# Computing each distance once in the position-bias stage of an attention and cos-gated FFN kernel

## The chip, the core and the metric

One core of a Trainium2 chip runs the whole program. The metric is the device time of one execution in microseconds (us); the kernel before has a median of 800.36 us over three runs (799.08 to 800.66).

The engines have short names in the profile: PE is TensorE's matmul, PEld its weight load, DVE is VectorE, ACT is ScalarE, POOL is GpSimd, SP is SyncE, which here only issues DMAs.

## What is computed

Attention with a learned bias that depends on the distance of two positions, then a feed-forward layer. S is 576, there are 8 heads and a batch of 4; all data are float32.

```
rel = pos[:, None] - pos[None, :]
psi_rel = log1p(abs(rel));  psi_i = log1p(max(pos[:, None], 1))
x = (psi_rel / psi_i)[..., None]
bias = max(x @ w1 + b1, 0) @ w2                  # 32 hidden values, 8 heads
scores = 0.125 * q @ k.T + bias
attn = softmax(scores);  y = attn @ v
h = y @ w_in;  out = (h * cos(h)) @ w_out
```

For a row i the bias depends on abs(i - j) alone, and on i by the factor 1 / psi_i.

## The kernel before

The program has three stages one after another: the bias stage, attention over 16 units (head pair and batch), and the feed-forward layer. The change touches the first alone.

**The bias stage** makes, for each row i and head, one line that holds the negative bias for every distance, and writes it to a scratch tensor `sc` in DRAM; attention reads it back (`load_bias`) at an offset that depends on the row. Rows go in 36 groups of 16. In the order of work groups 0 to 7 are rows 0 to 127 (t = 0), 8 to 15 the next 128 (t = 1), 16 to 19 the last 64 rows (t = 4), 20 to 27 and 28 to 35 the two tiles between (t = 2, 3); `qi` names a group by its rows, `k` (or `n` in the loop) by its place in this order. For group `qi` the distances forward reach `nf = 576 - 16 qi`, those backward `nr = 16 qi + 15`; together they are 591 columns, and the larger of the two, `n`, runs from 304 to 576.

A group has four subgroups `s` of four rows. Partitions hold 4 rows by 32 hidden values. For each `s`:

- one instruction makes the hidden values `ht` from the table `lt` of log1p(distance): on DVE (line 301, a multiply by the row's column `sl` of `st_` and a max against `nb1`), on POOL for `s == 2` of groups 8, 12, ... 32 (also line 301), or on ACT for `s == 3` of three groups in four (line 303, a Relu with a scale column and a bias column);
- TensorE multiplies by `nbd` (line 306). Its 32 output columns make it a matmul on one quarter of the array, `tile_position=(0, 32 * s)`, and its output goes to partitions 32 s to 32 s + 31 of the PSUM tile `pa`. The line is made in two or three pieces (`cuts`): the backward distances with a reversed operand, the forward ones as they are, and a further cut where a PSUM bank ends at 512 columns. Each float32 matmul runs as two passes, which the trace records as two matmuls with two weight loads.

When the four are done ACT adds a constant and writes the 591 columns from PSUM to `rt` (`bias_store`, line 318), and SP issues the DMA to `sc` (line 319).

Each engine runs its own instructions in the order in which the loop at line 328 writes them: group n's `ht` and matmuls, then the store of group n - 1, then, for n = 11 to 15, `turn`: transposes of the first unit's k and q on TensorE with copies out of PSUM on ACT (`kN`, `qT`, lines 195 to 212). POOL's queue also holds the splits of q and k (lines 172 and 176) at n = 1 and n = 16. Buffers tie the engines together: 2 PSUM tiles `pa` (each of two banks), 9 buffers for `ht`, 5 for `rt`.

Of the kernel before, what the change touches and what calls it, by code (L numbers as in the profile page):

```python
# [28 lines left out]
def kernel(  # L29
# [80 lines left out]
    with tc.manual_schedule():  # L110
# [152 lines left out]
        ha = opened(stage, "ha", 9, "left")  # L263
# [6 lines left out]
        st_ = ca.tile([128, S // 4], F32, name="st_")  # L270
        nb1 = ca.tile([128, 1], F32, name="nb1")
# [8 lines left out]
        nc.vector.tensor_scalar(st_, mi, w1c, None, ALU.mult)  # L280
        nc.vector.tensor_scalar(nb1, b1c, -1.0, None, ALU.mult)
# [6 lines left out]

        def bias_rows(k, t, gi):
# [4 lines left out]
            base = 512 - nr if max(nf, nr) <= 512 else 0  # L294
            cuts = sorted({0, nr, nr + nf} | ({512 - base} if base + nr + nf > 512 else set()))
            for s in range(4):
                ht = ha.tile([128, S], F32, tag="h", name="ht")
# [513 lines left out]
```

## Time and profile before

| what | value |
|---|---|
| median of three runs | 800.36 us |
| the profiled execution, its own time | 803.56 us |
| its span, first to last instruction | 801.7 us |
| granted TensorE clock over the span | 0.995 |
| PE, DVE, ACT, POOL busy | 764.9, 598.4, 459.1, 415.4 us |
| bias stage: first `ht`, last store starts | 4.80 and 79.54 us |
| attention, then feed-forward | to about 395, then to 801.7 us |

Busy times are those of the whole span. TensorE is busy for 95% of it, but its matmuls overlap, so the share doesn't tell how fast a stage goes; for the bias stage the distance between two stores `rt` is the better clock. The timeline merges instructions of the same line and tiles that follow each other closely into one row with a count. "idle before" names what the engine waited for.

### The profile page before, as it was taken

To read this page: it belongs to the slowest core of one execution; us is meant where nothing else is said; L and a number is where in the kernel's file an instruction comes from. 1 tells how busy PE (TensorE), PEld (TensorE's weight loads), DVE (VectorE), ACT (ScalarE), POOL (GpSimd) and SP (SyncE) were. 2 spreads that over 40 slices of the span, in tenths; PEclk is the share of its full clock that TensorE was granted. 3 is DMA by queue.
4 is the path that set the end of the run, shared out by engine and by line. 5 is a ranking of instruction groups with operands and counts; after the bars stand their busy time and mean duration, and the time that the engine had idled before them with its cause. 6 is when DMAs were issued, how large, how long until landed. Compare 5 with 4: busy or idle time off the path is not lost.

```text
span 801.7 us, 14168 instructions
## 1 busy us (share of the span) xinstructions
PE 764.9 (95%) x4882; PEld 619.2 (77%) x4882; DVE 598.4 (75%) x1300; ACT 459.1 (57%) x964; POOL 415.4 (52%) x493
## 2 busy tenths in 40 slices
PE   7899899989999999899999999999999999999997
PEld 4335677767777777677889998898888888889996
DVE  8558576757676767677577978889899898986655
ACT  5548677767777766676656555554544445443332
POOL 3324466656575657576753744637355373644400
PEclk9999999999999999999999999999999999999999
DMA  4647734673466346632001010111101011001112
GB/s 153 194 148 249 181 77 107 164 145 76 120 173 133 94 123 160 135 81 58 19 26 52 28 53 27 52 41 39 53 26 54 27 53 36 18 14 53 45 48 79
DMA packets 70599, 68.50 MB, mean 85 GB/s; under 512 B 30080, under 2 KB 54784, under 8 KB 70528
## 3 DMA queue, kind: packets, MB, share of 16 engines
q1 hardware_dynamic: 70528, 67.60, 31.1%
q8 instruction: 39, 0.64, 0.3%
q14 instruction: 32, 0.26, 0.1%
HBM read 42.00 MB, written 15.61 MB: 72 GB/s over the span
## 4 chain that ended last, share of the span: by engine, by line
PE 81%; ACT 7%; DMA 4%; DVE 4%; issue 3%; POOL 2%; SPq 0%; POOLq 0%; DVEq 0%; ACTq 0%
PE ph L613 24%; PE po L668 23%; PE pv L494 10%; PE s L378 8%; PE pa L306 7%; PE pt L437 4%; PE pt L195 3%; ACT P L408 3%; DMA bt<-sc 3%; POOL ht L301 1%; ACT kN L202 1%; PE pt L442 1%; ACT wb L91 1%; ACT PT L450 1%; DMA kS<-kN 1%
## 5 line engine op out<-in xcount | busy, mean ns | idle before, releaser
L430 POOL TENSOR_SCALAR P<-P,rc 128x576 f32<-128x576 f32 x144 | 111.1, 783 | 86.8 <-ACT PT L450 23.6
L389 DVE CUSTOM_DVE_ANT_0 neg<-s,bt 128x576 f32<-128x576 f32 x144 | 103.8, 753 | 37.4 <-PE s L378 33.3
L617 ACT ACTIVATE a<-ph,quarter 128x384 int32<-128x384 f32 x96 | 55.8, 581 | 106.6 <-PE ph L613 105.5
L408 ACT ACTIVATE P<-neg,m 128x576 f32<-128x576 f32 x144 | 110.6, 775 | 9.8 <-DVE dn L420 5.7
L480 POOL TENSOR_TENSOR xs<-xT,xs 128x384 fp32r<-128x384 f32 x96 | 107.7, 1122 | 8.0
L613 PE MATMUL ph<-xs,wpre 128*128 128x384 f32 x576 | 109.4, 338 | 0.8 <-DVE a L632 0.8
L613 PE MATMUL ph<-xs,w 128*128 128x384 f32 x576 | 108.3, 337 | 0.5 <-DVE a L632 0.5
L623 DVE SCALAR_TENSOR_TENSOR r<-a,ph 128x384 f32<-128x384 int32 x96 | 52.9, 551 | 73.1 <-ACT a L617 73.0
L613 PEld LDWEIGHTS ph<-xs,wpre 128*128 128x128 f32 x576 | 101.8, 188 | 6.2 <-DVE a L632 2.1
L613 PEld LDWEIGHTS ph<-xs,w 128*128 128x128 f32 x576 | 101.3, 188 | 5.6 <-DVE a L632 1.6
L628 ACT ACTIVATE r<-r,hpi 128x384 f32<-128x384 f32 x96 | 59.4, 619 | 69.4 <-DVE r L624 69.4
L378 PE MATMUL s<-kN,qT 128*128 128x288 f32 x320 | 94.3, 317 | 2.6 <-DVE dn L420 2.2
L378 PE MATMUL s<-kS,qT 128*128 128x288 f32 x320 | 87.1, 295 | 0.0
L437 PE MATMUL pt<-ident,P 128*128 128x128 f32 x576 | 80.7, 279 | 6.5 <-POOL P L430 6.4
L479 POOL TENSOR_SCALAR xs<-xT 128x384 fp32r<-128x384 f32 x96 | 62.0, 646 | 39.7 <-PE ph L613 39.7
L494 PE MATMUL pv<-PT,vN 128*64 128x320 f32 (+1 forms) x512 | 76.0, 419 | 0.0
L668 PE MATMUL po<-w,gh 128*128 128x512 f32 x288 | 75.3, 396 | 0.0
L668 PE MATMUL po<-wpre,gh 128*128 128x512 f32 x288 | 75.2, 396 | 0.0
L642 DVE TENSOR_TENSOR gl<-a,gh 128x384 fp32r<-128x384 f32 x96 | 74.4, 775 | 0.6 <-ACT gh L636 0.6
L306 PE MATMUL pa<-ht,nbd 128*32 128x79 f32 (+43 forms) x640 | 67.9, 419 | 6.1 <-POOL ht L301 3.6
L378 PEld LDWEIGHTS s<-kN,qT 128*128 128x128 f32 x320 | 60.9, 190 | 16.4 <-issue 9.7
L453 DVE COPY PT<-pt 128x512 f32<-128x512 f32 x64 | 43.8, 684 | 39.9 <-PE pt L437 39.8
(82 smaller groups left out, 1385.9 us busy)
## 6 DMA issues: line engine op xcount, KB each, us to landing
sc<-rt SPq DMA_DIRECT2D x36, 295.5 KB
kS<-kN SPq DMA_DIRECT2D x32, 304.0 KB
raw<-in_moe_w_in_dram SPq DMA_DIRECT2D x16, 512.0 KB
raw<-in_moe_w_out_dram SPq DMA_DIRECT2D x16, 512.0 KB
bt<-sc SPq DMA_DIRECT2D x16, 288.0 KB
nk<-in_k_dram SPq DMA_DIRECT2D x32, 128.0 KB
nq<-in_q_dram SPq DMA_DIRECT2D x32, 128.0 KB
vN<-in_v_dram SPq DMA_DIRECT2D x32, 128.0 KB
```

The lines of the kernel that those rows point to most:

```text
L306: nc.tensor.matmul(ps[32 * s : 32 * s + 32, base + a : base + b], nbd, rhs, start=True, stop=True, tile_position=(0, 32 * s),)
L378: nc.tensor.matmul(s[:, hf, 0:HALF], a, kt[u][:, c0 : c0 + HALF], start=(n == 0), stop=(n == 2 * len(stats) - 1),)
L389: nc.vector.tensor_tensor_reduce(neg, s[:, :, 0:HALF], bias[hp, t, h].rearrange("p (a x) -> p a x", a=2), 1.0, 3.0e38, ALU.add, ALU.min, m ...
L408: nc.scalar.activation(out=P[u, j][:, 576 * h : 576 * h + 576], in_=neg.rearrange("p a x -> p (a x)"), func=AF.Exp, bias=m[:, 0:1], scale= ...
L430: nc.gpsimd.tensor_scalar(p, p, r, 1.0, ALU.mult, ALU.mult)
L437: nc.tensor.transpose(ps[:, 128 * c : 128 * c + 128], p[:, o : o + 128], ident)
L479: nc.gpsimd.tensor_scalar(h, src, 1.0, 1.0, ALU.mult, ALU.mult)
L480: nc.gpsimd.tensor_tensor(l, src, f(h), ALU.subtract)
L494: nc.tensor.matmul(ps[64 * h : 64 * h + 64, 0 : WQ[hf]], a, m, start=(c == 0), stop=(c == 4), tile_position=(0, 64 * h), skip_group_check= ...
L613: nc.tensor.matmul(ps, a, x, start=(i == 0), stop=(i == 3 * KD - 1))
L642: nc.vector.tensor_tensor(gl, a, f(G[key][0]), ALU.subtract)
L668: nc.tensor.matmul(O[n][i], a[:, 128 * i : 128 * i + 128], w, start=(i0 == 0 and p == 0), stop=(i0 == GF - 1 and p == 2),)
```

## The change

Since a row's factor 1 / psi_i is positive, it can be taken out of the activation: max(w1 x + b1, 0) becomes the factor times max(w1 lt + b1 psi_i, 0). The change uses this:

- `lt` is multiplied by w1 once. The hidden values need one limit per row, `edge` (or `nedge` on ACT), in place of a factor and a limit: DVE and POOL run a max with one column (line 313), ACT a Relu with a bias column (line 315).
- TensorE computes columns 0 to n - 1 alone, each distance once, in one piece, or two where n is over 512 (line 318).
- `bias_store` runs two activations, forward and reversed, on the same PSUM columns, with the row's factor as the scale column `mrow` and the constant as the bias column (line 334).
- ACT makes `ht` for `s == 3` of every second group instead of three in four; DVE makes the others.
- At the start DVE computes `edge`, `nedge` and `mrow`; `mrow` needs four small matmuls with a selection matrix `pick`.
- `ht` has 8 buffers instead of 9.

```diff
-        ha = opened(stage, "ha", 9, "left")
+        ha = opened(stage, "ha", 8, "left")
...
-        nc.vector.tensor_scalar(st_, mi, w1c, None, ALU.mult)
-        nc.vector.tensor_scalar(nb1, b1c, -1.0, None, ALU.mult)
+        nc.vector.reciprocal(nedge, mi)
+        nc.vector.tensor_scalar(nedge, nedge, b1c, None, ALU.mult)
+        nc.vector.tensor_scalar(edge, nedge, -1.0, None, ALU.mult)
+        nc.vector.tensor_scalar(lt, lt, w1c, None, ALU.mult)
...
+        nc.vector.tensor_copy(
+            pick.rearrange("p (g h) -> p g h", g=4), ident[:, 0:128:32].unsqueeze(2).to_broadcast([128, 4, 8])
+        )
+        pm = bank()
+        for s in range(4):
+            nc.tensor.matmul(
+                pm[32 * s : 32 * s + 32, 0:NQ], pick, mi[:, s : 4 * NQ : 4], start=True, stop=True, tile_position=(0, 32 * s)
+            )
+        nc.vector.tensor_copy(mrow, pm[:, 0:NQ])
...
-                if s < 3 or k % 4 == 2:
+                o = 4 * qi + s
+                if s < 3 or k % 2:
                     eng = nc.gpsimd if s == 2 and k in POOL_H else nc.vector
-                    eng.tensor_scalar(ht[:, 0:n], lt[:, 0:n], sl, nb1, ALU.mult, ALU.max)
+                    eng.tensor_scalar(ht[:, 0:n], lt[:, 0:n], edge[:, o : o + 1], None, ALU.max)
                 else:
-                    nc.scalar.activation(out=ht[:, 0:n], in_=lt[:, 0:n], func=AF.Relu, scale=sl, bias=b1c)
-                for a, b in zip(cuts[:-1], cuts[1:]):
-                    rhs = ht[:, nr - a : nr - b : -1] if b <= nr else ht[:, a - nr : b - nr]
+                    nc.scalar.activation(out=ht[:, 0:n], in_=lt[:, 0:n], func=AF.Relu, bias=nedge[:, o : o + 1])
+                for a in range(0, n, 512):
+                    b = min(a + 512, n)
...
-            nc.scalar.activation(out=rt[:, 0 : RB - 1], in_=ps, func=AF.Identity, bias=cst[:, int(k % 4 == 2) : int(k % 4 == 2) + 1])
+            c = cst[:, k % 2 : k % 2 + 1]
+            for o, i in ((rt[:, nr : nr + nf], ps[:, 0:nf]), (rt[:, 0:nr], ps[:, nr:0:-1])):
+                nc.scalar.activation(out=o, in_=i, func=AF.Identity, scale=mrow[:, qi : qi + 1], bias=c)
```

Three places of the order show what the diff alone doesn't. TensorE's queue at group 16, the first of t = 4, with the transposes of q ahead of it, before:

```order
L195 MATMUL pt_548<-identr_64,sq_211 128x128 x4
L306 MATMUL pa_554<-ht_555,nbd_136 32x512 [waits DVE_49,PE_49,Activation_49]
L306 MATMUL pa_554<-ht_555,nbd_136 32x15
L306 MATMUL pa_554<-ht_555,nbd_136 32x64
L306 MATMUL pa_554<-ht_560,nbd_136 32x512 [waits DVE_49]
L306 MATMUL pa_554<-ht_560,nbd_136 32x15
```

and now:

```order
L195 MATMUL pt_510<-identr_64,sq_215 128x128 x4
L318 MATMUL pa_516<-ht_517,nbd_136 32x512 [waits DVE_49,PE_49,Activation_49]
L318 MATMUL pa_516<-ht_517,nbd_136 32x16
L318 MATMUL pa_516<-ht_521,nbd_136 32x512 [waits DVE_49]
L318 MATMUL pa_516<-ht_521,nbd_136 32x16
L318 MATMUL pa_516<-ht_525,nbd_136 32x512 [waits Pool_49]
```

A subgroup had three pieces here (six passes in the trace) and has two (four passes). In groups 4 to 15 and 20 to 35 it had two and has one.

ACT's queue around the copies of k (n = 11 and 12), before:

```order
L318 ACTIVATE rt_430<-pa_393,cst_137 128x591 [waits DMAHW3_49,PE_49,Activation_49]
L202 ACTIVATE kN_438<-pt_439 128x2x2x128 [waits PE_49]
L303 ACTIVATE ht_458<-lt_132,pk_133,st__134 128x384 [waits DVE_49]
L318 ACTIVATE rt_462<-pa_413,cst_137 128x591 [waits DMAHW4_49,Activation_49]
L202 ACTIVATE kN_438<-pt_465 128x2x2x128 [waits PE_49]
L211 ACTIVATE kN_438<-pt_471 128x128 [waits PE_49]
L212 ACTIVATE kN_438<-pt_471 128x64
L303 ACTIVATE ht_491<-lt_132,pk_133,st__134 128x368 [waits DVE_49]
L318 ACTIVATE rt_495<-pa_445,cst_137 128x591 [waits DMAHW5_49,Activation_49]
```

and now:

```order
L334 ACTIVATE rt_403<-pa_373,cst_137,mrow_154 128x416 [waits DMAHW3_49,PE_49]
L334 ACTIVATE rt_403<-pa_373,cst_137,mrow_154 128x175
L202 ACTIVATE kN_412<-pt_413 128x2x2x128 [waits PE_49]
L315 ACTIVATE ht_429<-lt_132,nedge_135 128x384 [waits Activation_49]
L334 ACTIVATE rt_432<-pa_390,cst_137,mrow_154 128x400 [waits DMAHW4_49]
L334 ACTIVATE rt_432<-pa_390,cst_137,mrow_154 128x191
L202 ACTIVATE kN_412<-pt_436 128x2x2x128 [waits PE_49]
L211 ACTIVATE kN_412<-pt_442 128x128 [waits PE_49]
L212 ACTIVATE kN_412<-pt_442 128x64
L334 ACTIVATE rt_462<-pa_419,cst_137,mrow_154 128x384 [waits DMAHW5_49]
L334 ACTIVATE rt_462<-pa_419,cst_137,mrow_154 128x207
```

Each store is two rows; the `ht` of group 13 (368 columns) is no longer between the copies and the next store, DVE makes it.

DVE's queue from the arrival of `pack` to the second `ht`, before:

```order
L280 TENSOR_SCALAR st__134<-pk_133 128x144 [waits DMAHW0_49]
L281 TENSOR_SCALAR nb1_135<-pk_133 128x1
L282 TENSOR_SCALAR nbd_136<-pk_133 128x32
L285 MEMSET cst_137 128x2
L286 TENSOR_SCALAR cst_137<-pt_157 96x1 [waits DVE_49,PE_49]
L287 TENSOR_SCALAR cst_137<-pt_157 128x1
L301 TENSOR_SCALAR ht_163<-lt_132,st__134,nb1_135 128x576 [waits DMAHW1_49]
L301 TENSOR_SCALAR ht_168<-lt_132,st__134,nb1_135 128x576
```

and now:

```order
L282 RECIPROCAL nedge_135<-pk_133 128x144 [waits DMAHW0_49]
L283 TENSOR_SCALAR nedge_135<-nedge_135,pk_133 128x144 [waits DVE_49]
L284 TENSOR_SCALAR edge_134<-nedge_135 128x144 [waits DVE_49]
L285 TENSOR_SCALAR lt_132<-lt_132,pk_133 128x576 [waits DMAHW1_49]
L286 TENSOR_SCALAR nbd_136<-pk_133 128x32
L289 MEMSET cst_137 128x2
L290 TENSOR_SCALAR cst_137<-pt_161 96x1 [waits DVE_49,PE_49]
L291 TENSOR_SCALAR cst_137<-pt_161 128x1
L293 COPY pick_155<-ident_63 128x32
L301 COPY mrow_154<-pt_167 128x36 [waits PE_49]
L313 TENSOR_SCALAR ht_174<-lt_132,edge_134 128x576
L313 TENSOR_SCALAR ht_178<-lt_132,edge_134 128x576
```

Seven instructions stand between the arrival of `lt` and the first `ht`, one of them behind a wait for TensorE.

## Rows read from the trace of the kernel before

**Rows 1.** Busy time by stretch: PE, PEld, DVE, ACT, POOL (instructions), clock, DMA share, GB/s

```profile
4.80:24.60 19.80, 16.17 (x168) 9.82 (x168) 18.03 (x34) 11.51 (x16) 10.97 (x7) 1.00 0.48 154
24.60:43.35 18.75, 18.05 (x146) 8.41 (x147) 11.15 (x23) 10.84 (x21) 6.22 (x4) 0.91 0.64 212
43.35:56.61 13.26, 13.26 (x98) 4.69 (x100) 5.57 (x11) 5.02 (x8) 2.49 (x3) 1.00 0.28 95
56.61:79.55 22.94, 22.32 (x257) 11.46 (x247) 20.19 (x43) 18.34 (x28) 9.26 (x6) 1.00 0.71 249
```

**Rows 2.** Timeline of ACT, the stores of groups 8, 15 and 19: start, duration

```profile
26.56 0.75 ACT L318 ACTIVATE rt<-pa,cst 128x591 f32<-128x591 f32 x1 [4.30 <-issue]
...
43.35 0.74 ACT L318 ACTIVATE rt<-pa,cst 128x591 f32<-128x591 f32 x1
...
56.61 0.75 ACT L318 ACTIVATE rt<-pa,cst 128x591 f32<-128x591 f32 x1 [2.27 <-issue]
```

**Rows 3.** Timeline of TensorE's weight loads in group 16

```profile
42.88 0.17 PEld L306 LDWEIGHTS pa<-ht,nbd 128*32 128x32 f32 x5 [0.32 <-issue]
43.34 0.11 PEld L306 LDWEIGHTS pa<-ht,nbd 128*32 128x32 f32 x1 [0.29 <-issue]
43.77 0.17 PEld L306 LDWEIGHTS pa<-ht,nbd 128*32 128x32 f32 x5 [0.32 <-issue]
```

**Rows 4.** Timeline of TensorE's matmuls in group 14: start, time to the last one's end

```profile
37.43 1.22 PE L306 MATMUL pa<-ht,nbd 128*32 128x239 f32 x16
```

**Rows 5.** Groups of instructions by shape, 0 to 110 us: busy us, mean ns of one

```profile
L318 ACT ACTIVATE rt<-pa,cst 128x591 f32<-128x591 f32 x36 | 27.0, 751 | 24.2 <-PE pa L306 11.0 <-issue 9.8 <-ACT ht L303 1.8
L408 ACT ACTIVATE P<-neg,m 128x576 f32<-128x576 f32 x14 | 10.8, 772 | 3.5 <-DVE m L389 2.7 <-DVE dn L420 0.8
L303 ACT ACTIVATE ht<-lt,pk,st__134 128x576 f32<-128x576 f32 x2 | 1.7, 862 | 2.7 <-DMA lt<-in_ltab_dram 2.7
L303 ACT ACTIVATE ht<-lt,pk,st__134 128x320 f32<-128x320 f32 x2 | 1.3, 642 | 0.0
L301 DVE TENSOR_SCALAR ht<-lt,st__134,nb 128x576 f32<-128x576 f32 x6 | 3.3, 579 | 1.7 <-DMA lt<-in_ltab_dram 0.9 <-PE pa L306 0.8
L301 DVE TENSOR_SCALAR ht<-lt,st__134,nb 128x304 f32<-128x304 f32 x7 | 2.9, 438 | 4.9 <-PE pa L306 4.9
L306 PE MATMUL pa<-ht,nbd 128*32 128x335 f32 x8 | 1.5, 457 | 0.0
L306 PE MATMUL pa<-ht,nbd 128*32 128x336 f32 x8 | 1.5, 446 | 0.0
```

**Rows 6.** Timeline of ACT, store and hidden values back to back

```profile
15.17 0.75 ACT L318 ACTIVATE rt<-pa,cst 128x591 f32<-128x591 f32 x1
15.82 0.79 ACT L303 ACTIVATE ht<-lt,pk,st__134 128x496 f32<-128x496 f32 x1
```

**Rows 7.** Timeline of ACT, the copies of k in groups 11 and 12

```profile
31.60 0.66 ACT L202 ACTIVATE kN<-pt 128x512 fp32r<-128x512 f32 x1 [1.08 <-PE pt L195]
...
34.56 0.65 ACT L202 ACTIVATE kN<-pt 128x512 fp32r<-128x512 f32 x1 [1.09 <-PE pt L195]
```

**Rows 8.** Timeline of POOL, hidden values of groups 8 and 32, split of k

```profile
18.76 5.81 POOL L301 TENSOR_SCALAR ht<-lt,st__134,nb 128x448 f32<-128x448 f32 x1 [7.18 <-ACT rt L318]
...
42.52 1.89 POOL L176 TENSOR_TENSOR sk<-nk,sk 128x320 fp32r<-128x320 f32 x2
...
71.44 2.45 POOL L301 TENSOR_SCALAR ht<-lt,st__134,nb 128x464 f32<-128x464 f32 x1 [3.60 <-DVE ht L301]
```

**Rows 9.** Timeline of DVE from the arrival of `pack`

```profile
3.06 0.30 DVE L280 TENSOR_SCALAR st__134<-pk 128x144 f32<-128x144 f32 x1 [0.71 <-DMA pk<-in_pack_dram]
...
4.80 18.03 DVE L301 TENSOR_SCALAR ht<-lt,st__134,nb 128x576 f32<-128x576 f32 x34 [0.88 <-DMA lt<-in_ltab_dram]
```

**Rows 10.** DVE's reciprocals in attention: ns min/median/max

```profile
L423 DVE RECIPROCAL rc<-dn x80: 162/166/168, 83.9 to 386.1; 128x2 f32<-128x2 f32 x64, 128x1 f32<-128x1 f32 x16
```

**Rows 11.** Chain that ended last: start, us, what

```profile
87.38 6.89 DMA bt<-sc
```

More of the change, by code (lines that the diff above doesn't have):

```diff
@@ L269 @@
         pk = ca.tile([128, pack.shape[1]], F32, name="pk")
-        st_ = ca.tile([128, S // 4], F32, name="st_")
-        nb1 = ca.tile([128, 1], F32, name="nb1")
+        edge = ca.tile([128, S // 4], F32, name="edge")
+        nedge = ca.tile([128, S // 4], F32, name="nedge")
         nbd = ca.tile([128, 32], F32, name="nbd")
@@ L279 @@
         bd, w2r = pk[:, 146:178], pk[0:C, 178:306]
-        nc.vector.tensor_scalar(st_, mi, w1c, None, ALU.mult)
-        nc.vector.tensor_scalar(nb1, b1c, -1.0, None, ALU.mult)
+        mrow = ca.tile([128, NQ], F32, name="mrow")
+        pick = ca.tile([128, 32], F32, name="pick")
+        nc.vector.reciprocal(nedge, mi)
+        nc.vector.tensor_scalar(nedge, nedge, b1c, None, ALU.mult)
+        nc.vector.tensor_scalar(edge, nedge, -1.0, None, ALU.mult)
+        nc.vector.tensor_scalar(lt, lt, w1c, None, ALU.mult)
         nc.vector.tensor_scalar(nbd, bd, -1.0, None, ALU.mult)
@@ L293, in bias_rows @@
             ps = ps_a.tile([128, 1024], F32, tag="a", name="pa")
-            base = 512 - nr if max(nf, nr) <= 512 else 0
-            cuts = sorted({0, nr, nr + nf} | ({512 - base} if base + nr + nf > 512 else set()))
             for s in range(4):
                 ht = ha.tile([128, S], F32, tag="h", name="ht")
-                sl = st_[:, 4 * qi + s : 4 * qi + s + 1]
-                if s < 3 or k % 4 == 2:
+                o = 4 * qi + s
+                if s < 3 or k % 2:
                     eng = nc.gpsimd if s == 2 and k in POOL_H else nc.vector
-                    eng.tensor_scalar(ht[:, 0:n], lt[:, 0:n], sl, nb1, ALU.mult, ALU.max)
+                    eng.tensor_scalar(ht[:, 0:n], lt[:, 0:n], edge[:, o : o + 1], None, ALU.max)
                 else:
-                    nc.scalar.activation(out=ht[:, 0:n], in_=lt[:, 0:n], func=AF.Relu, scale=sl, bias=b1c)
-                for a, b in zip(cuts[:-1], cuts[1:]):
-                    rhs = ht[:, nr - a : nr - b : -1] if b <= nr else ht[:, a - nr : b - nr]
+                    nc.scalar.activation(out=ht[:, 0:n], in_=lt[:, 0:n], func=AF.Relu, bias=nedge[:, o : o + 1])
+                for a in range(0, n, 512):
+                    b = min(a + 512, n)
                     nc.tensor.matmul(
-                        ps[32 * s : 32 * s + 32, base + a : base + b],
+                        ps[32 * s : 32 * s + 32, a:b],
                         nbd,
-                        rhs,
+                        ht[:, a:b],
                         start=True,
@@ L313, in bias_rows @@
                     )
-            return ps[:, base : base + nr + nf]
+            return ps
         def bias_store(k, t, gi, ps):
+            qi = groups[t][gi]
+            nf, nr = S - 16 * qi, 16 * qi + 15
             rt = ra.tile([128, RB], F32, tag="r", name="rt")
-            nc.scalar.activation(out=rt[:, 0 : RB - 1], in_=ps, func=AF.Identity, bias=cst[:, int(k % 4 == 2) : int(k % 4 == 2) + 1])
+            c = cst[:, k % 2 : k % 2 + 1]
+            for o, i in ((rt[:, nr : nr + nf], ps[:, 0:nf]), (rt[:, 0:nr], ps[:, nr:0:-1])):
+                nc.scalar.activation(out=o, in_=i, func=AF.Identity, scale=mrow[:, qi : qi + 1], bias=c)
             nc.sync.dma_start(out=sc[t][gi, :, 0 : RB - 1], in_=rt[:, 0 : RB - 1])
```

## The prediction

> **What bounds the stage now.** I read the busy time by stretch first, cut mostly at stores [rows 1, 2]. The reader is to see four different rates. From the first `ht` to 24.6 us DVE is busy for 18.03 of 19.80 us. Groups 8 to 15 take 16.8 us (26.56 to 43.35). Groups 16 to 19 take 13.26 us, 3.3 us each, with DVE, ACT and the DMAs at half load or less and TensorE busy throughout. Groups 20 to 35 take 22.94 us, 1.43 us each, with DVE and ACT both at 80% or more.
>
> Then the rows inside. In groups 16 to 19 each subgroup starts 0.89 us after the last one [rows 3]: the first pass of its 512 columns takes 0.46 us (42.88 to 43.34), the second as long, and the next subgroup, on another quarter of the array, doesn't begin before. In group 14, whose subgroups have two pieces, 16 passes of all four quarters run in 1.22 us [rows 4]; one subgroup alone needs 2 x 591 x 0.9 ns = 1.06 us (price below). So quarters do run side by side, and in groups 16 to 19 they don't. What differs is six passes per subgroup against four: I read it as a queue that holds about four matmuls of a quarter, so that the fifth and sixth block those of the next quarter until the two long passes are over.
>
> In groups 11 to 15 ACT waits: copy of k to copy of k is 2.96 us [rows 7]. The copy waits for transposes, these for the group's last matmuls, these for the `ht` that stands on ACT's queue behind the copy before.
>
> **The change part by part.** Prices first.
>
> - One pass costs 0.46/512 = 0.9 ns a column. A group falls from 591 columns to n, 440 on average; a subgroup alone from 1.06 us to 0.8.
> - ACT: 220 columns of `ht` (862 to 642 ns) are 0.86 ns each [rows 5]. 576 columns cost 862 ns with two column operands and 772 with one (another function, so an estimate): 0.09 us an operand. Back to back, a store is issued 0.65 us before the next instruction [rows 6], 0.10 less than its duration. A store's fixed part is 751 - 591 x 0.86 = 243 ns. Two activations with one more operand each cost 2 x (0.243 + 0.09 - 0.10) + 0.51 = 0.97 us a group, against 0.65. An `ht` of ACT falls to 0.47 us (320 columns) to 0.66 (560), and there are 18 instead of 27.
> - DVE: 438 ns at 304 columns and 579 at 576 give 0.52 ns a column and 280 fixed [rows 5]; with one column operand 296 ns at 144 [rows 9] leave 221. So 59 ns less each, 119 instead of 110 instructions: 54 against 56 us in all. This costs nothing beside ACT's work, which is now the longer queue in most groups.
> - POOL: no row has a max with one operand. With a multiply and a max it takes 2.45 us at 464 columns [rows 8]; I take this as unchanged. One operand less is a gain if anything, and lies in the bounds below.
>
> *Start and groups 0 to 7: +0.7 us.* Ahead of the first `ht` come a reciprocal, three multiplies, `pick`, four matmuls and `mrow`. The reciprocal at 144 columns is bounded by [rows 10]: one and two columns lie within 6 ns, so at most 166 + 144 x 6 = 1.0 us. With two short multiplies it ends near 4.6, under the wait for `lt`, which lands at 4.8 [rows 9]. Behind that wait stand `lt` times w1 (0.5), five short ones (0.5) and matmuls with a copy (0.7): the first `ht` comes 1.7 us later. DVE makes 28 of these groups' `ht` against 26, each 0.06 shorter than its 18.03/34 = 0.53 us [rows 9], and regains most of 1 us. Then POOL's `ht` of group 8, which took 5.81 us while DVE ran without a gap [rows 8], stalls TensorE as before. Bounds: -1 to +2.
>
> *Groups 8 to 15: -3.9 us.* I add up ACT's queue from the store of group 8 to that of group 15: seven stores 6.8, four `ht` (10, 12, 14, 16) 2.2, the copies 2.6, four waits for transposes of 0.35 each: 13.0 against 16.8. Only groups 12 and 14 still need an `ht` of ACT behind a copy. Bounds: -5 (no waits) to -2 (one 2.96 us turn fewer, nothing else).
>
> *Groups 16 to 19: -7.0 us.* Four passes a subgroup; quarters run side by side, about 1.0 us a group. ACT then sets the pace: four stores 3.9, two `ht` 1.2, 0.2 of waits: 5.3 us. POOL's split of k (its larger part 1.89 us [rows 8]) ran beside an idle DVE and now falls beside DVE's work; I add 1.0. So 6.3 against 13.26. Bounds: -8 to -4.5 (POOL's `ht` of group 20 late by the 2.45 us of [rows 8]).
>
> *Groups 20 to 35: -0.5 us.* ACT: 16 stores 15.5, seven `ht` of 0.54: 19.3. POOL's late `ht` and the split of q cost about 2.5 to 3 as they do now. 22.4 against 22.94. Bounds: -2.5 to +2.
>
> *After the stage: +0.3 us* for the longer last store. The wait for the bias read at 87.38 [rows 11] hangs on SP's order after the stage and moves with it. The buffer taken from `ht` costs nothing: with eight, a subgroup reuses the buffer of two groups ago, still the two groups that PSUM allows.
>
> The sum is 0.7 - 3.9 - 7.0 - 0.5 + 0.3 = -10.4 us. The profiled execution took 803.56 us, 0.4% over the median, and would come to 793.2; the median 800.36 comes to **790.0 us**.
>
> **Rows and the skill.** The 16 passes of group 14 [rows 4] overlap across quarters, so a later subgroup starts before an earlier one has ended. The Trainium skill, "TensorE: Matmul & The Clock Gate", Part 3, says that matmuls start and end strictly in program order. The trace disagrees in group 14 and looks like it in group 16; by the page the 7.0 us would not come, which is the first rival.
>
> **The rivals.**
>
> 1. *A long piece in front still holds the next quarter* (slower). If what blocks in group 16 is the 512-column piece followed by a short one in the next bank, and not the count of passes, then groups 16 to 19 keep their 13.26 us and groups 0 to 3 (512 and 64 to 16 columns) get the same 0.89 us a subgroup: 3.55 us against 1.72 (3.25 `ht` of DVE at 0.53), +7.3. Sum: 0.7 + 7.3 - 3.9 - 0.5 + 0.3 = +3.9, **804 us**. It decides if the next quarter's first pass waits for the second long pass. Against it: in group 14 the longer forward piece ran beside the others. Chance 0.07.
> 2. *ACT reads PSUM backwards slowly.* The reversed line has 295 columns a group on average. No row has ACT reading backwards; TensorE reads `ht` backwards from SBUF at 457 ns for 335 columns against 446 forwards for 336 [rows 5]. At half rate it adds 295 x 0.86 = 0.25 us to each of the 28 groups that ACT paces, 7 us: **797 us**. At 2.5 times the cost per column the gain is gone. On reading, the Trainium skill, "Advanced Engine Details and Errata", PSUM Cachelines, wants every two consecutive elements contiguous for best throughput; no run here shows whether a step of -1 counts as that. Chance 0.09.
> 3. *TensorE's clock falls to its lower level*, since it works only about 0.8 of each 1.3 us. After the idle stretch ahead of 24.6 us the second stretch has 0.91 granted [rows 1]. At 1.2 GHz a column takes twice the 0.9 ns, so 440 take 2 x 440 x 1.8 ns = 1.6 us a group and pace groups 8 to 35 instead of ACT: +0.25 each, **797 us**. In groups 16 to 19 one quarter worked at a time and the clock stayed at 1.00, which speaks against it. Chance 0.1.
> 4. *POOL starves.* If DVE, no longer held up by TensorE, leaves it no gap, its `ht` of groups 12, 16 and 20 take 5.8 us as that of group 8 did, some 2 us late each: **796 us**. Chance 0.08.
>
> **How the numbers follow.** The forecast has 0.63, the rivals 0.34, a gain lost in a way I don't name 0.03. The forecast's own terms, with their bounds half used, give 786 to 794; the range reaches on through rivals 2 to 4, to 798.5, and to 785. It leaves out rival 1 and gains beyond 15 us. A difference of 0.2% (1.6 us) is about what a measurement of this kernel can tell from none. Slower by that: rival 1 and the far end of rival 2, 0.09. Within it: 0.06. Faster: 0.85.
>
> **What would show it.** Right: in the stretch of t = 4 stores 1.3 to 1.7 us apart and all four quarters starting within a few tens of ns; a store pair of about 1.0 us; the store of group 15 some 3 us earlier and that of group 19 some 10; first `ht` near 6.5 us; attention as long as now. Wrong: subgroups still 0.89 us apart (rival 1), a reversed activation longer than its forward twin per column (2), a granted clock under 0.95 after 30 us (3), `ht` of POOL over 4 us in groups 12 to 20 (4).

## The result and the profile after

The median went from 800.51 us (799.08 to 803.9, four runs) to **792.12 us** (790.13 to 795.37, four runs). The ratio is 0.9893 with a 95% interval of 0.9854 to 0.9931. The forecast was 790.0, with a range of 785.0 to 798.5.

The profiled execution after took 792.59 us with a span of 790.8 us and a granted clock of 0.994. Its span is 10.9 us shorter than that of before. Not all of that is the change: the wait for the last bias tile at the start of attention ends at 94.27 us before [rows 11] and at 85.94 after, 8.3 us earlier, which agrees with the medians (8.4). What follows it differs by up to 6 us between executions of kernels with the same attention: from the `neg` that waits there to the span's end 701.8 us in e5 below, 707.8 in e3. So the stage is read at fixed points of the trace here, and the run by its ratio.

Busy time by stretch after, from the first `ht` on, cut at the stores of groups 8, 15, 19 and 35 (PE, PEld, DVE, ACT, POOL with instructions, clock, DMA share, GB/s):

```profile
6.48:23.87 17.39, 15.99 (x110) 6.19 (x112) 17.29 (x37) 10.63 (x20) 7.53 (x7) 1.00 0.43 140
23.87:37.01 13.14, 10.64 (x84) 3.55 (x78) 9.91 (x24) 12.01 (x26) 4.95 (x4) 1.00 0.79 234
37.01:43.34 6.33, 5.58 (x67) 2.59 (x61) 5.22 (x12) 5.34 (x12) 2.33 (x3) 1.00 0.82 309
43.34:71.09 27.75, 20.02 (x129) 4.61 (x124) 20.04 (x50) 20.25 (x40) 6.81 (x6) 0.94 0.64 222
```

Beside [rows 1, 2]: the store of group 8 starts 2.7 us earlier, groups 8 to 15 take 13.14 us instead of 16.79, groups 16 to 19 take 6.33 instead of 13.26, and groups 20 to 35 take 27.75 instead of 22.94. In the last stretch no engine is busy for more than 73% and the DMAs have 0.64: something else is waited for.

ACT's timeline after shows it (start, duration; in brackets the idle time ahead and what ended it):

```profile
37.01 1.09 ACT L334 ACTIVATE rt<-pa,cst,mrow 128x336 f32<-128x336 f32 x2
38.58 1.08 ACT L334 ACTIVATE rt<-pa,cst,mrow 128x64 f32<-128x64 f32 x2 [0.48 <-DMA sc<-rt]
...
43.34 1.08 ACT L334 ACTIVATE rt<-pa,cst,mrow 128x16 f32<-128x16 f32 x2
...
53.22 1.08 ACT L334 ACTIVATE rt<-pa,cst,mrow 128x256 f32<-128x256 f32 x2 [3.55 <-DMA sc<-rt]
...
60.47 1.09 ACT L334 ACTIVATE rt<-pa,cst,mrow 128x192 f32<-128x192 f32 x2 [1.57 <-DMA sc<-rt]
...
71.09 1.09 ACT L334 ACTIVATE rt<-pa,cst,mrow 128x80 f32<-128x80 f32 x2 [0.48 <-PE pa L318]
```

A store may begin when one of the five `rt` is free, that is when the write to `sc` from it has landed. Twice ACT stands still for that, 6.4 us in all with the short ones. The waits of SP's queue (engine, line, what it waited for: us, times, longest) and the chain of waits (start, us, what) tell what the writes do:

```profile
SPq L252 <- DMA sc<-rt: 4.0, 1, 4.0
SPq L239 <- DMA sc<-rt: 2.0, 2, 1.4
```

```profile
38.12 6.55 DMA sc<-rt
46.78 6.36 DMA sc<-rt
54.36 6.02 DMA sc<-rt
79.02 6.92 DMA bt<-sc
```

A bias load reads what the writes of its row tile left, so SP waits at it until the last of those has landed, and the writes of later groups stand behind it. Before, with groups 16 to 19 at 3.3 us each, the four groups between a tile's last write and its load gave enough time, and SP waited for no write. Now a write takes 6.0 to 6.6 us from issue to landing, and four groups take as long.

### The profile page after: what moved, and what is told of

Its sections match the earlier page's. It is cut to its first block, busy times and chain, and to the rows that moved or that the text cites. A ratio compares the mean times of both kernels' runs of the same rounds, so it can differ in the third digit from the quotient of the medians.

```text
span 790.8 us, 13558 instructions
## 1 busy us (share of the span) xinstructions
PE 747.6 (95%) x4602; PEld 601.9 (76%) x4602; DVE 597.2 (76%) x1313; ACT 462.2 (58%) x991; POOL 407.5 (52%) x493
## 4 chain that ended last, share of the span: by engine, by line
PE 77%; ACT 8%; DMA 6%; DVE 3%; issue 3%; POOL 1%; SPq 1%; POOLq 0%; DVEq 0%; ACTq 0%
PE ph L629 25%; PE po L684 24%; PE pv L510 10%; PE s L394 8%; PE pt L453 4%; PE pt L195 3%; ACT P L424 3%; DMA sc<-rt 2%; PE pa L318 2%; DMA bt<-sc 2%; ACT kN L202 1%; PE pt L458 1%; ACT wb L91 1%; DMA nk<-in_k_dram 1%; ACT rt L334 1%
## 5 line engine op out<-in xcount | busy, mean ns | idle before, releaser
L453 PEld LDWEIGHTS pt<-ident,P 128*128 128x128 f32 x576 | 62.1, 142 | 8.2 <-POOL P L446 5.7
```

The lines of the kernel that those rows point to most:

```text
L453: nc.tensor.transpose(ps[:, 128 * c : 128 * c + 128], p[:, o : o + 128], ident)
```

## The experiments

All times of the table are starts in one profiled execution of each kernel: the stores of groups 8, 15, 19 and 35, ACT's waits for writes to `sc` up to 90 us, and the second `neg` of the last bias tile (attention's first unit), which waits for the last bias load (in e6 the first one does, to 92.60). The last column is the ratio to the kernel before on the same chip with its interval; e5, e6 and e9 ran once, for their trace, and have the one time taken.

| kernel | 8 | 15 | 19 | 35 | waits | `neg` | ratio or us |
|---|---|---|---|---|---|---|---|
| before | 26.56 | 43.35 | 56.61 | 79.54 | none | 94.44 | 1 |
| changed | 23.87 | 37.01 | 43.34 | 71.09 | 6.4 | 86.10 | 0.9893 (0.9854 to 0.9931) |
| e11, changed again | 24.00 | 37.15 | 44.54 | 70.52 | 4.2 | 85.75 | 0.9888 (0.9861 to 0.9916) |
| e3, three pieces | 23.91 | 37.00 | 50.58 | 74.32 | 2.3 | 89.66 | 0.9940 (0.9913 to 0.9968) |
| e4, before in turn | 27.03 | 43.53 | 49.28 | 75.30 | 3.3 | 90.20 | 0.9939 (0.9909 to 0.9970) |
| e8, limit only | 23.01 | 38.84 | 52.16 | 75.85 | 1.6 | 91.24 | 0.9952 (0.9929 to 0.9975) |
| e5, POOL two | 24.48 | 37.59 | 44.45 | 70.52 | 4.7 | 85.63 | 789.17 |
| e9, DVE two | 28.53 | 42.62 | 48.62 | 75.89 | 4.8 | 90.80 | 797.56 |
| e1, loads later | 24.06 | 37.18 | 42.88 | 67.91 | 4.5 | 85.27 | 0.9873 (0.9841 to 0.9906) |
| e2, seven `rt` | 23.92 | 37.03 | 42.73 | 66.69 | 3.2 | 83.50 | 0.9880 (0.9830 to 0.9929) |
| e6, loads after | 24.00 | 37.16 | 42.87 | 64.58 | none | 94.81 | 800.99 |
| e7, loads moved | 23.93 | 37.04 | 44.67 | 69.30 | 3.8 | 84.28 | 0.9916 (0.9892 to 0.9941) |
| e10, early k | 24.07 | 37.20 | 44.76 | 72.44 | 7.0 | 87.67 | 0.9894 (0.9866 to 0.9923) |
| e12, ACT at the start | 24.44 | 37.53 | 44.13 | 71.02 | 4.9 | 85.62 | 0.9914 (0.9893 to 0.9935) |

### Groups 16 to 19: passes or columns (e3, e4)

e3 puts the third piece back into the changed kernel, with no column more:

```diff
-                for a in range(0, n, 512):
-                    b = min(a + 512, n)
+                cuts = [0, 512, 512 + (n - 512) // 2, n] if t == 4 else [*range(0, n, 512), n]
+                for a, b in zip(cuts[:-1], cuts[1:]):
```

> The changed kernel, but in groups 16 to 19 the columns behind 512 are made in two matmuls instead of one: three pieces, six passes a subgroup, as in the kernel before, with no column more. Theory A (a quarter's queue holds about four matmuls): subgroups start 0.8 to 0.9 us apart, a group takes 3.3 us, groups 16 to 19 take 12 to 13.3 us instead of 6.33, ACT's later waits for sc<-rt shrink, and the whole run is 3 to 6 us longer than the changed kernel: 795 to 798. Rival (the 7 us came from fewer columns and one backward piece less, not from the count of passes): the stretch stays at 6.3 to 7.5 us, 792 to 793.

e4 leaves the kernel before its 591 columns and three pieces, and lets the four quarters take turns in these groups:

```diff
+            hts = []
             for s in range(4):
...
-                for a, b in zip(cuts[:-1], cuts[1:]):
+                hts.append(ht)
+            pieces = list(zip(cuts[:-1], cuts[1:]))
+            for s, (a, b) in [(s, p) for p in pieces for s in range(4)] if t == 4 else [(s, p) for s in range(4) for p in pieces]:
+                    ht = hts[s]
```

> The kernel before, but in groups 16 to 19 TensorE runs the first piece of all four subgroups, then the second, then the third, with the same 591 columns. Theory A (a quarter's queue holds about four matmuls, so two passes of each quarter in turn never block): groups 16 to 19 take 6 to 8 us instead of 13.26; the bias loads then meet the same waits as in the changed kernel and give 2 to 4 us back in groups 20 to 35: 794 to 798. Rival (fewer columns are what made these groups fast): 13 us as before, 800 to 801.

ACT's timeline of e3, the stores of groups 15 to 20:

```profile
37.00 1.10 ACT L334 ACTIVATE rt<-pa,cst,mrow 128x336 f32<-128x336 f32 x2
39.90 1.09 ACT L334 ACTIVATE rt<-pa,cst,mrow 128x64 f32<-128x64 f32 x2 [1.80 <-PE pa L318]
43.46 1.09 ACT L334 ACTIVATE rt<-pa,cst,mrow 128x48 f32<-128x48 f32 x2 [1.82 <-PE pa L318]
47.02 1.09 ACT L334 ACTIVATE rt<-pa,cst,mrow 128x32 f32<-128x32 f32 x2 [2.47 <-PE pa L318]
50.58 2.06 ACT L334 ACTIVATE rt<-pa,cst,mrow 128x16 f32<-128x16 f32 x4 [2.02 <-PE pa L318]
```

and that of e4, the stores of groups 15 to 19:

```profile
43.53 0.74 ACT L322 ACTIVATE rt<-pa,cst 128x591 f32<-128x591 f32 x1
45.02 0.75 ACT L322 ACTIVATE rt<-pa,cst 128x591 f32<-128x591 f32 x1
46.36 0.76 ACT L322 ACTIVATE rt<-pa,cst 128x591 f32<-128x591 f32 x1 [0.59 <-PE pa L310]
47.77 0.75 ACT L322 ACTIVATE rt<-pa,cst 128x591 f32<-128x591 f32 x1
49.28 0.75 ACT L322 ACTIVATE rt<-pa,cst 128x591 f32<-128x591 f32 x1 [0.22 <-ACT ht L304]
```

e3 takes 13.58 us for the four groups (13.26 before), e4 takes 5.75 us with all the columns. Theory A held in both, with the one a little above its range and the other a little below. TensorE's weight loads show the pattern, first in e3 (group 16), then in the changed kernel (the last two of group 16 and those of group 17; group 16 itself had to wait for its fourth `ht`):

```profile
37.82 0.17 PEld L318 LDWEIGHTS pa<-ht,nbd 128*32 128x32 f32 x5 [0.32 <-issue]
38.28 0.11 PEld L318 LDWEIGHTS pa<-ht,nbd 128*32 128x32 f32 x1 [0.29 <-issue]
38.71 0.17 PEld L318 LDWEIGHTS pa<-ht,nbd 128*32 128x32 f32 x5 [0.32 <-issue]
```

```profile
38.06 1.27 PEld L318 LDWEIGHTS pa<-ht,nbd 128*32 128x32 f32 x17 [0.32 <-issue]
```

In e3 a burst of five and one alone alternate every 0.89 us, as in [rows 3]; in the changed kernel the loads of a whole group run through in 1.27 us. So these 7 us come from the sequence of a quarter's matmuls and not from fewer columns: the change happened to fall from six passes in a row to four. e4 also shows that the kernel before could have had them by order alone; it too gives 3.1 us back in groups 20 to 35 (26.02 against 22.94).

The count of passes alone doesn't do it. In groups 0 to 3 of the kernel before a subgroup has six passes in a row as well, but with the short piece first and a shorter long one (63, 449 and 79 columns in group 3). There the stores of groups 2 and 3 are 1.53 us apart, where quarters that hold each other would need some 3.2 us (an estimate: 4 x 2 x 449 columns at the prediction's 0.9 ns):

```profile
13.64 0.75 ACT L318 ACTIVATE rt<-pa,cst 128x591 f32<-128x591 f32 x1 [0.61 <-PE pa L306]
15.17 0.75 ACT L318 ACTIVATE rt<-pa,cst 128x591 f32<-128x591 f32 x1
```

What is shown to hold the next quarter is a third piece behind a long first one. A queue from which the two short passes are gone before it is full would fit both; no run tests the order of the pieces by itself.

### The start: the limit operand (e8, e5, e9)

e8 is the changed kernel with TensorE's 591 columns, one store a group and ACT's share of `ht` as before:

```diff
+            base = 512 - nr if max(nf, nr) <= 512 else 0
+            cuts = sorted({0, nr, nr + nf} | ({512 - base} if base + nr + nf > 512 else set()))
...
-                if s < 3 or k % 2:
+                if s < 3 or k % 4 == 2:
...
-                for a in range(0, n, 512):
-                    b = min(a + 512, n)
+                for a, b in zip(cuts[:-1], cuts[1:]):
+                    rhs = ht[:, nr - a : nr - b : -1] if b <= nr else ht[:, a - nr : b - nr]
...
-            for o, i in ((rt[:, nr : nr + nf], ps[:, 0:nf]), (rt[:, 0:nr], ps[:, nr:0:-1])):
-                nc.scalar.activation(out=o, in_=i, func=AF.Identity, scale=mrow[:, qi : qi + 1], bias=c)
+            nc.scalar.activation(out=rt[:, 0 : RB - 1], in_=ps, func=AF.Identity, scale=mrow[:, qi : qi + 1], bias=c)
```

> Half of the change: hidden values by one limit operand, with the row factor as the scale column of the store, and the start with the reciprocal; but TensorE computes all 591 columns with reversed pieces as in the kernel before, one store a group, and ACT makes ht for three groups in four. Theory A (the 3.4 us that the start gave beyond the prediction come from the limit operand alone, through POOL's ht of group 8 and DVE): the store of group 8 starts at 23.5 to 24.5 us as in the changed kernel; groups 16 to 19 still take 13 to 13.5 us; the run is 2 to 3 us shorter than the kernel before, 0.996 to 0.998. Rival (they come from TensorE's shorter work): the store of group 8 starts at 26 us or later, and the run takes as long as the kernel before or longer.

Its store of group 8 starts at 23.01 us, 3.55 earlier than before although its first `ht` comes 1.7 later, and groups 16 to 19 take 13.32 us. Theory A held, with the store 0.5 us ahead of its range; the run gave 0.9952, a little more than expected. Groups 8 to 15 take 15.84 us in e8, so 0.95 of the 3.65 us that the change gains there come without fewer columns and without the second store; the rest wasn't taken apart.

e5 gives POOL's `ht` a second column operand again (`ones` is a column of ones). e9 has the same lines with the two calls exchanged, so that DVE's have it:

```diff
-                    eng = nc.gpsimd if s == 2 and k in POOL_H else nc.vector
-                    eng.tensor_scalar(ht[:, 0:n], lt[:, 0:n], edge[:, o : o + 1], None, ALU.max)
+                    if s == 2 and k in POOL_H:
+                        nc.gpsimd.tensor_scalar(ht[:, 0:n], lt[:, 0:n], ones, edge[:, o : o + 1], ALU.mult, ALU.max)
+                    else:
+                        nc.vector.tensor_scalar(ht[:, 0:n], lt[:, 0:n], edge[:, o : o + 1], None, ALU.max)
```

> The changed kernel, but POOL makes its seven ht with two column operands, a multiply by a column of ones and then the max. Theory A (an operand less is what made POOL fast: 1.2 to 2.6 us instead of 1.9 to 5.8): its ht take 2.0 to 2.6 us at 304 to 528 columns and 4 to 6 us at group 8, where DVE runs without a gap; the store of group 8 starts at 26 to 27.5 us instead of 23.87. Rival (POOL was slow before because DVE's own two-operand instructions held it up, and DVE is short now): POOL's ht stay within 0.3 us of the changed kernel's, the store of group 8 starts within 0.5 us of 23.87.

> The changed kernel, but DVE makes its ht with two column operands, a multiply by a column of ones and then the max, while POOL keeps one. It is the other half of the run in which POOL had two. Theory A (two column operands on DVE's instructions are what held POOL's ht of group 8 up to 5.81 us in the kernel before): POOL's ht of group 8 takes 4 to 6 us instead of 2.56, the store of group 8 starts at 26 us or later, and a DVE ht takes 50 to 60 ns more. Rival (group 8's POOL ht was slow only when both engines had two operands): POOL's ht of group 8 stays under 3.2 us, and the store of group 8 comes at 24.5 to 26 us, later by DVE's own 37 x 0.06 us alone.

POOL's timeline, its `ht` of group 8, in the changed kernel, in e5 and in e9:

```profile
20.24 2.56 POOL L313 TENSOR_SCALAR ht<-lt,edge 128x448 f32<-128x448 f32 x1 [8.62 <-PE pa L318]
```

```profile
20.43 2.98 POOL L315 TENSOR_SCALAR ht<-lt,ones,edge 128x448 f32<-128x448 f32 x1 [8.63 <-PE pa L322]
```

```profile
21.53 5.17 POOL L315 TENSOR_SCALAR ht<-lt,edge 128x448 f32<-128x448 f32 x1 [9.23 <-PE pa L322]
```

With two on both engines it is the 5.81 us of [rows 8]. e9's theory A held. e5's held for POOL's other six `ht` (1.92 to 2.68 us against 1.23 to 1.81) and fell for that of group 8; its rival fell too.

Where the time of group 8 goes is seen beside POOL's instruction: DVE's busy time from POOL's start to DVE's first pause, and behind it, in the kernel before, e9, the changed kernel and e5 (stretch, length, DVE's busy time with instructions, clock, DMA share, GB/s):

```profile
18.76:22.82 4.06, 4.06 (x10) 1.00 0.53 163
22.83:24.57 1.74, 0.00 (x0) 1.00 0.56 160
```

```profile
21.53:25.42 3.89, 3.89 (x10) 1.00 0.60 166
25.43:26.70 1.27, 0.00 (x0) 0.72 0.63 181
```

```profile
20.24:21.30 1.06, 1.06 (x3) 1.00 0.27 103
21.30:21.40 0.10, 0.00 (x1) 1.00 1.09 378
```

```profile
20.43:21.47 1.04, 1.04 (x3) 1.00 0.25 93
21.48:21.56 0.08, 0.00 (x0) 1.00 1.04 355
```

| column operands | POOL's start to DVE's first pause | from there to POOL's end |
|---|---|---|
| one on each (changed) | 1.06 | 1.5 |
| two on POOL (e5) | 1.04 | 1.9 |
| two on DVE (e9) | 3.89 | 1.3 |
| two on each (before) | 4.06 | 1.7 |

With two operands DVE runs ten instructions without a gap before it has to wait for TensorE; with one its instructions are shorter, it catches up with TensorE after three and stands for 0.1 us. POOL's `ht` ends 1.3 to 1.9 us after that pause in all four. So POOL's own operand costs 0.4 us here, and DVE's costs the pause. It doesn't slow POOL by itself: in groups 12, 16 and 20 of e9 POOL's `ht` take 1.43, 1.88 and 1.54 us, against 1.37, 1.81 and 1.35 in the changed kernel. That POOL waits for the pause is read from these traces; no run sets the pause alone. The store of group 8 then waits for POOL's `ht`, in e9:

```profile
28.53 1.08 ACT L338 ACTIVATE rt<-pa,cst,mrow 128x448 f32<-128x448 f32 x2 [4.28 <-PE pa L322]
```

The Trainium skill, "SBUF — State Buffer", "SBUF: two separate sides", says that VectorE and GpSimd share one pair of ports, which certain instructions of the one hold to their end while the other waits. That fits an `ht` of POOL that grows while DVE leaves no gap. It doesn't tell why POOL got in at none of the changes from one of the ten DVE instructions to the next, and no run here does.

### Groups 20 to 35: what holds the writes (e1, e2, e6, e7, e10)

e1 changes one number, e2 the buffers (with `bp` 9 instead of 10 and `tt` 3 instead of 4 for room):

```diff
-            if n >= 4 and todo[n - 4][1] == len(groups[todo[n - 4][0]]) - 1:
-                load_bias(0, todo[n - 4][0])
+            if n >= 8 and todo[n - 8][1] == len(groups[todo[n - 8][0]]) - 1:
+                load_bias(0, todo[n - 8][0])
```

> The changed kernel, but SP issues the bias loads of a row tile eight groups after the tile's last group instead of four. Theory A (SP's order): in the changed kernel SP waits 6.0 us in all at the bias loads for the scratch writes ahead of them (4.0 at line 252, 2.0 at line 239), the stores behind them are issued late, the five rt buffers run out, and ACT waits 6.4 us. With eight groups between, the writes have landed: SP's waits for sc<-rt and ACT's waits for sc<-rt both fall under 1.5 us, groups 20 to 35 take 22 to 23.5 us instead of 27.75, the whole run is 4 to 5 us shorter than the changed kernel's 792.1: 787 to 788. Theory B (the DMAs' throughput): writes come faster than they land whatever the order; groups 20 to 35 stay at 26 to 28 us, 791 to 793. Theory C (ACT or DVE pace these groups at their new rate): ACT's waits go, and waits for PE or ht take their place; 26 us or more.

```diff
-        ra = opened(stage, "ra", 5, "left")
+        ra = opened(stage, "ra", 7, "left")
```

> The changed kernel with seven rt buffers instead of five; the room comes from one buffer each of the bias tiles and of attention's neg, so the time after the stage may differ and the stage is read from the trace. Theory A: two buffers more cover two groups, 2 x 1.2 us of each of the two long waits (3.55 and 1.57 us), so ACT's waits for sc<-rt fall from 6.4 to 1.5 to 3 us and groups 20 to 35 take 23.5 to 25 us; SP still waits about 6 us at the bias loads. Theory B: the waits only come later; ACT's waits stay over 5 us, 27 to 28 us. Theory C: as A for the waits, but the stretch stays at 27 us.

e6 takes the loads out of the loop and issues them behind the last store:

> The changed kernel, but all bias loads are issued behind the last store of the stage, so that SP has nothing but the scratch writes, the swap of k and early loads between groups 8 and 35. The time after the stage gets longer and is not compared. Theory A (SP's wait at the loads, and the loads themselves, hold the writes up): ACT's waits for sc<-rt fall from 6.4 to under 1 us, the last store starts at 64 to 66.5 us instead of 71.09. Rival (a write lands some 6.5 us after its issue, and five buffers in 6.5 us allow one store in 1.3 us, whatever SP does): ACT still waits 3 to 5 us for sc<-rt and the last store starts at 67.5 to 70.

The waits fall on one group or another from execution to execution (the changed kernel itself took 27.75 us for groups 20 to 35 in its first profile and 25.98 in e11), so the stores of groups 15 and 35 are the better ends. From the one to the other the changed kernel takes 34.08 us (33.37 in e11), e1 30.73, e2 29.66 and e6 27.42. In e6 ACT waits for no write, and the stretch is a little shorter than the 6.3 and 22.4 us that the prediction had worked out from ACT's queue. So theory A of e6 held, and what the changed kernel lost are the bias loads among the writes, 6.0 to 6.7 us. Part of that may be SP standing at them: in e1, where SP waits for no write between 37 and 75 us, 2.6 to 3.4 us come back. The rest is not: in e1 ACT still waits 4.5 us for writes, and in e10 below, where SP waits for none either, 7.0. In e2 SP stands at the loads for 7.8 us, and two more buffers cover half of ACT's waits (3.2 us are left, just over theory A's 3). Theory A of e1 was right in its direction and too large, and for the whole run wrong: the 3.2 us by which its stage ends earlier turn up again at the start of attention. DVE's timeline, the two `neg` of the last tile, after and in e1:

```profile
82.89 0.76 DVE L405 CUSTOM_DVE_ANT_0 neg<-s,bt 128x576 f32<-128x576 f32 x1 [1.54 <-DMA bt<-sc]
...
86.10 0.76 DVE L405 CUSTOM_DVE_ANT_0 neg<-s,bt 128x576 f32<-128x576 f32 x1 [2.45 <-DMA bt<-sc]
```

```profile
82.79 0.76 DVE L405 CUSTOM_DVE_ANT_0 neg<-s,bt 128x576 f32<-128x576 f32 x1 [4.62 <-DMA bt<-sc]
85.27 0.76 DVE L405 CUSTOM_DVE_ANT_0 neg<-s,bt 128x576 f32<-128x576 f32 x1 [1.72 <-DMA bt<-sc]
```

Of 3.2 us 0.8 arrive; of e2's 4.4 us 2.6 arrive, and its run isn't shorter beyond its interval. e7 and e10 go for that wait by order: e7 with six groups between and the last tile's load ahead of the load of k and the swap of k, e10 with six groups between and the load of k for unit 2 issued at group 20.

```diff
+        load_bias(0, tiles[-1])
         stage.close()
...
-            if i == 1:
-                load_bias(0, tiles[-1])
```

> The changed kernel, but the bias loads of a row tile come six groups after its last group instead of four, and those of the last tile right behind the last store, ahead of the load of k, the swap of k and the weight load that stand before them now. Theory A (order on SP's queue sets when the bias lands): the last store starts at 67.5 to 69 us, the last bias tile lands 3 to 5 us earlier than at 86.1, the run takes 787 to 789.5 us, 0.983 to 0.986 of the kernel before. Rival (the DMAs have too much to move between 40 and 86 us, whatever the order): the second neg of the last tile still starts at 84.5 to 86.5, 791 to 794 us, 0.988 to 0.991.

```diff
             if n == 16:
                 split(1, "k")
+            if n == 20:
+                load(2, "k")
```

> The changed kernel, with the bias loads six groups behind instead of four, and the load of k for unit 2 issued at group 20 instead of at the start of attention, so that fewer transfers stand beside and ahead of the last bias tile; the swap of k stays ahead of it and POOL's splits keep their place. Theory A (order at the start of attention sets when the last bias tile lands): the last store starts at 67.5 to 69.5 us, the last tile's second neg starts at 82 to 84 us instead of 86.1, unit 1 isn't late, and the run is 2 to 4 us shorter than the changed kernel on the same chip. Rival (too much to move): 85 to 86.5 us, and within 1.5 us of the changed kernel.

Neither theory A held, and the second `neg` (84.28 and 87.67) lies outside both rivals' ranges too. e7's last tile comes 1.8 us earlier, but the swap of k for unit 1 now stands behind it, and unit 1's first `neg` starts late, waiting for scores:

```profile
84.28 0.76 DVE L406 CUSTOM_DVE_ANT_0 neg<-s,bt 128x576 f32<-128x576 f32 x1 [3.23 <-DMA bt<-sc]
92.64 0.76 DVE L406 CUSTOM_DVE_ANT_0 neg<-s,bt 128x576 f32<-128x576 f32 x1 [2.71 <-PE s L395]
```

In e10 the load of k joins the writes, ACT's waits for them are 7.0 us, and the stage ends 1.4 us later than in the changed kernel. Over the changed kernel and these four the second `neg` stays between 83.5 and 87.7 us, wherever the waits lie. Whether that is the DMAs' throughput or the time of each transfer stays open: their share between 37 and 86 us is 0.72 in the changed kernel and 0.68 to 0.77 in e1, e2, e7 and e10, not full.

### More of ACT at the start (e12, e11)

```diff
-                if s < 3 or k % 2:
+                if s < 3 or k % 2 and k > 8:
```

The constant's column in `bias_store` changes with it.

> The changed kernel, but ACT makes the fourth ht of every one of the groups 0 to 8 instead of every second, where DVE runs without a gap (17.29 of 17.39 us) and ACT is busy for 10.63. Theory A (the stage's early part is worth its time, since everything behind it starts earlier): four ht of DVE less are 4 x 0.46 = 1.8 us, the store of group 8 starts at 22 to 22.5 us instead of 23.87, and the last bias tile and the run come 1 to 2 us earlier than in the changed kernel, 0.986 to 0.988 of the kernel before. Rival (the transfers between 37 and 86 us set when attention gets its last bias tile, whatever comes ahead): the store of group 8 comes earlier by the same 1.8 us, but the last tile's second neg starts within 0.7 us of 86, and the ratio stays at 0.989.

> The changed kernel itself once more, on the chip of these runs, as the measure for the others. Its ratio to the kernel before lies in 0.985 to 0.993 as in the first result; the store of group 8 starts within 0.3 us of 23.87 and the last one within 0.5 us of 71.09.

Neither theory's first step came: e12's stores of groups 1 to 7 follow each other in 1.5 to 1.6 us, because ACT with a store and an `ht` in every group now paces them, and group 8 isn't earlier. So the question that it was made for is still open. e11 repeats the changed kernel's ratio within its interval; its last store is 0.57 us earlier, a little more than the 0.5 expected. No version here beats it by more than the intervals.

## Why the prediction was right, and which terms were not

The sum was -10.4 us and the medians show -8.4. Its five terms, by the stores of the profiled execution and, for the last, the second `neg`:

| term | predicted | measured |
|---|---|---|
| start and groups 0 to 7 | +0.7 | -2.7 |
| groups 8 to 15 | -3.9 | -3.65 |
| groups 16 to 19 | -7.0 | -6.93 |
| groups 20 to 35 | -0.5 | +4.8 |
| after the stage | +0.3 | +0.1 |

- **Groups 16 to 19** went as reasoned in what carries the gain, four passes a subgroup and then ACT's pace. That 6.33 us meet the 6.3 so closely is luck. The 1.0 us added for POOL's split did not come; in its place ACT waits 0.48 and 0.51 us for writes to `sc` (at 38.58 and 40.82). Without such waits e1, e2 and e6 take 5.70 us, with longer ones (0.88 and 1.16) e11 takes 7.39. The reading of six passes against four rested on one pattern; e3 and e4 show it from both sides. As a plain count it is too wide: six passes with the short piece first held nothing in groups 0 to 3. The first rival (a long piece followed by a short one holds the next quarter) is refuted by the burst of 17 weight loads in 1.27 us. The Trainium skill, "TensorE: Matmul & The Clock Gate", Part 3, has matmuls start and end strictly in program order. By that each subgroup of the changed kernel would start behind the long passes of the one ahead, 0.89 us later as before; the burst of 1.27 us for a whole group disagrees, for quarters of the array.
- **Groups 8 to 15** went as reasoned: the copies of k start at 27.91 and 30.44 us after, 2.53 apart instead of 2.96 [rows 7], and a pair of stores takes 1.08 us, 0.98 from issue to issue (0.97 predicted).
- **The start** failed in one step: "POOL's `ht` of group 8, which took 5.81 us while DVE ran without a gap [rows 8], stalls TensorE as before". It took 2.56, and the store of group 8 follows that of group 7 after 1.88 us instead of 5.68. The prediction looked for POOL's price in POOL's operands; e5 and e9 show that most of it lay in whether DVE makes a pause. e8, with the limit operand and no fewer columns, gives a start term of -3.55. The other steps held: the first `ht` is at 6.48 (6.5 predicted), the reciprocal takes 1.05 us (by [rows 10] at most 1.03, rounded to 1.0), and the store of group 7 is 1.1 us late where the sum had 0.7:

```profile
3.03 1.05 DVE L282 RECIPROCAL nedge<-pk 128x144 f32<-128x144 f32 x1 [0.68 <-DMA pk<-in_pack_dram]
...
6.48 18.27 DVE L313 TENSOR_SCALAR ht<-lt,edge 128x576 f32<-128x576 f32 x38
```

The store of group 7, before and after:

```profile
20.88 0.75 ACT L318 ACTIVATE rt<-pa,cst 128x591 f32<-128x591 f32 x1
```

```profile
21.99 1.08 ACT L334 ACTIVATE rt<-pa,cst,mrow 128x464 f32<-128x464 f32 x2
```

- **Groups 20 to 35** failed in a step that isn't there: the sum took ACT's queue (22.4 us) and nothing of the writes and loads that the faster groups bring closer together, although [rows 1] show the DMA share there at 0.71 with 1.43 us a group. The measured +4.8 us (+3.0 in e11) lie outside its bounds of -2.5 to +2. e6, with the loads out of the way, takes 21.71 us from the store of group 19 to that of 35: the price of ACT was right, the missing term was the loads among the writes.

These two misses are 3.4 and 5.3 us of opposite sign. That they nearly cancel is luck, and the time came out near the forecast partly by it; the mechanism that carries the gain, the passes of groups 16 to 19, was right.

How much of the gain is due to the saved columns themselves stays open. e4, by order alone, has 0.9939, and e8, by the limit operand alone, 0.9952. Multiplied, as an estimate, that is 0.989, the changed kernel's ratio; no run has these two and nothing else, and the intervals are some 0.003 to either side.

Rival 2 is refuted by ACT's groups by shape: the reversed activation of 575 or 559 columns takes what its forward twin takes.

```profile
L334 ACT ACTIVATE rt<-pa,cst,mrow 128x576 f32<-128x576 f32 x1 | 0.8, 830 | 5.3 <-PE pa L318 5.3
L334 ACT ACTIVATE rt<-pa,cst,mrow 128x559 f32<-128x559 f32 x1 | 0.8, 821 | 0.0
L334 ACT ACTIVATE rt<-pa,cst,mrow 128x575 f32<-128x575 f32 x1 | 0.8, 819 | 0.0
L334 ACT ACTIVATE rt<-pa,cst,mrow 128x560 f32<-128x560 f32 x1 | 0.8, 817 | 0.7 <-PE pa L318 0.7
```

Rival 3 came for a stretch: behind the wait of 3.55 us, in which TensorE stood for 3.83 us (to 54.36), the granted clock was 0.62, so TensorE ran at the lower of its two levels, 1.2 GHz, for most of it. Over groups 20 to 35 it was 0.94, just under the sign that the prediction gave.

```profile
53.22:56.50 3.28, 2.14 (x12) 0.75 (x16) 0.67 (x2) 2.78 (x6) 0.52 (x1) 0.62 0.54 190
56.50:60.47 3.97, 3.24 (x24) 0.45 (x16) 3.51 (x10) 2.40 (x5) 0.90 (x1) 0.88 0.76 278
```

ACT waited 0.50 us for TensorE there (at 56.32), which is the most that it cost in these two stretches. Rival 4 didn't come: POOL's `ht` of groups 12, 16 and 20 took 1.37, 1.81 and 1.35 us.

## What to carry to other kernels

When a stage gets faster, ask again of every wait that was covered by its slowness: here a load that reads back what a stage writes came four groups later, which was 13 us and became 6, as long as a write takes to land. Work on one engine can hang on its neighbour's pauses: POOL's `ht` took 5.17 us beside ten DVE instructions without a gap and 2.56 where DVE stood for 0.1 us after three. Where two changes come at once, look which of them pays: the 7 us of groups 16 to 19 could be had by the order of the matmuls alone. A gain inside a stage counts only where the next stage's first wait moves with it; three kernels here ended the stage 1.8 to 4.4 us earlier and none made the run shorter beyond its interval.

## What the runs showed of the hardware

- Six passes in a row on one quarter of the array, the two of 512 columns first, hold the other quarters' matmuls (0.89 us a subgroup); four in a row let a group's four subgroups run in about 1.3 us, and six taken in turn by quarter let four groups pass in 5.75 us (e3, e4). Six with the short piece first held nothing (stores 1.53 us apart in the kernel before). That a quarter's queue holds about four is a reading of these.
- POOL's `ht` of group 8 ended 1.3 to 1.9 us after the first pause of the DVE instructions beside it, whether that came after 1.06 or after 4.06 us (changed kernel, e5, e9, before); POOL's own second operand added 0.4.
- Reading PSUM backwards costs ACT nothing (819 ns for 575 columns against 830 for 576).
